# VectorE takes the absolute value in the first step of four batches: an S4D and token-mixing block on one Trainium2 core

## The chip, the cores and the metric

The kernel runs on one core of a Trainium2 chip. The metric is device time in microseconds, the median of several runs. The engines go by the names of the profile: PE is TensorE's matmul and PEld its weight load, DVE is VectorE, ACT is ScalarE, POOL is GpSimd, and SP issues most of the DMAs. Each engine works off its own instructions in program order and waits on semaphores for the others.

## The reference

The block normalizes its input, runs it through a long convolution whose kernel comes from a state-space model (S4D), and then through a token-mixing MLP. Cut to what matters:

```python
def _A_ref(u, log_A_real, A_imag, C_real, C_imag, log_dt, D_skip):   # L = 2048, D = 448, N = 256
    dt = jnp.exp(log_dt)
    A = -jnp.exp(log_A_real) + 1j * A_imag
    C = (C_real + 1j * C_imag) * dt[:, None]
    P = jnp.exp((A * dt[:, None])[:, :, None] * pos[None, None, :])
    K = 2.0 * jnp.einsum("dn,dnl->dl", C, P).real
    Kf = jnp.fft.rfft(K, L2)
    Uf = jnp.fft.rfft(u_t, L2)
    y = jnp.fft.irfft(Uf * Kf[None, :, :], L2)[:, :, :L]
    ...
    return y + u * D_skip[None, None, :]

x = x + ga * _A_ref(layernorm(x) * (1 + ca) + sa, ...)
h = layernorm(x) * (1 + cb) + sb
x = x + gb * mixer(h)        # layernorm, w1 over the tokens, gelu, w2 over the tokens
```

The change lies in the making of K and in the products of the spectra.

## The kernel before

K is made in 56 steps (`NHALF`). A step is one half (128 of the 256 states) of a group of 16 channels. For each step PE makes exponents (`st_exponents`) and later phases, in turns (`st_phase`), each as two PSUM tiles `xe` and `xg` of 128 x 512. ACT takes Exp of the exponents into `mag` (`st_exp`), and sines and cosines of the phases (`st_step`). A cosine is Sin(pi/2 - 2 pi |phase|), so it needs the absolute phase: `ab` from `xe` and one of the three buffers `gs` (`cg_`) from `xg`. Sin of `xe` is written over `xe` itself, after `ab` has been read from it; the cosine of `xe`'s phases goes into `xg`. From these, POOL multiplies the two halves of `G` (L734, L735), and DVE the four quarters of `E`: L736 and L737 with the sine (in the program one half of `E`), L739 and L740 with the cosine (the other half). PE sums `G` times `E` over the states into `kg` (`st_kgen`).

Exp and Sin need different tables on ACT, and a table is loaded by an instruction of its own in front of the first function that needs it. So the steps go in seven batches of 8 (`BATCH`). A batch begins with a window (`window`, from step 40 on `late_window`): eight times Exp, with the next exponents on PE, and other work put in between. Then its eight steps use Sin. The table load for Sin stands in the first step of a batch, behind the two Abs (the first batch loads it at the end of its window). `xe` and `xg` have two buffers each, so the phase of step s + 2 can be made once step s has read its own for the last time (L740).

What else the steps carry:

- `chain(q)` prepares the parameters of 128 channels (the last, q = 3, of 64) as a row of small DVE instructions. `more(n)` issues n of them: in windows by the table `WPACE` (a row for each window, an entry for each of its eight Exp), in steps by `pace`, through `between()`, which stands between the two halves of `E` and first issues what waits in the list `dve`.
- `st_s1` takes finished sums to the first transform on PE (`y1`); its two copies into `yk` go into a list and are issued by `flush`.
- `u_cols` transforms the input's columns for the spectrum (`pu` on PE, `uo` on DVE, then DMAs).
- `piece` works on one piece of the product of spectra: `pc_s2` makes `kx` on PE, `pc_mul` multiplies it on DVE with the input's spectrum `u` into `z` (two instructions, L877), `pc_inv` transforms back on PE (`vv`). In steps 40 and 48, `piece(True)` stands ahead of `st_step` and `piece(False, True)` behind it. `warm` issues ten matmuls on PE whose results nobody reads.

PE, ACT, DVE and POOL run in the order in which the program is written. SP's DMAs are put in order by the tile framework until step 56.

Of the kernel before, what the change touches and what calls it, by code (L numbers as in the profile page):

```python
# [11 lines left out]
F32 = mybir.dt.float32  # L12
F32R = mybir.dt.float32r
BF16 = mybir.dt.bfloat16
AF = mybir.ActivationFunctionType
ALU = mybir.AluOpType
# [6 lines left out]
P = 128  # L23
# [209 lines left out]
def tile_adaln_s4d_mixer(ctx, tc, i, out):  # L233
    nc = tc.nc
    x = i["A_u"][0]
# [17 lines left out]
    with ExitStack() as es:  # L253
        V, S, G, T = nc.vector, nc.scalar, nc.gpsimd, nc.tensor
        tt, ts, stt = V.tensor_tensor, V.tensor_scalar, V.scalar_tensor_tensor
# [126 lines left out]
        def flush(todo):  # L382
            while todo:
                todo.pop(0)()
# [321 lines left out]
        def st_mag2(s):  # L706
            me = v32(mags[s][:, 0])
            w = wp.tile([P, GD], F32, tag="w", name="w")
            G.tensor_tensor(w[:, :, None], me[:, :, 31:32], me[:, :, 1:2], ALU.mult)
            if s in (3, 4, 5):  # L710
                m2 = v32(wm0.rearrange("p k d -> p (k d)")[:, -512 * (s - 2) :][:, 0:512])
            else:
                m2 = m2p[s >= 32 and s % BATCH > 2].tile([P, GD, 32], F32, tag="m2", name="m2")
            G.tensor_tensor(m2, me, w[:, :, None].to_broadcast([P, GD, 32]), ALU.mult)  # L714
            m2s[s] = m2

        def st_step(s, between):
            me, mg_, m2 = v32(mags[s][:, 0]), v32(mags[s][:, 1]), m2s.pop(s)
            E = gp_.tile([P, 2, GD, NJ], F32, tag="E", name="E")
            Gt = gp_.tile([P, 2, GD, NI], F32, tag="G", name="G")  # L720


            xe, xg = phs.pop(s)
            ab, sg, cg_ = (wp.tile([P, 512], F32, tag=nm, name=nm, bufs=b) for nm, b in (("ab", 1), ("gs", 3), ("gs", 3)))

            S.activation(ab, xe, AF.Abs)
            S.activation(cg_, xg, AF.Abs)
            flush(due)
            S.activation(xe, xe, AF.Sin, scale=TWO_PI)
            S.activation(sg, xg, AF.Sin, scale=-TWO_PI)  # L730
            S.activation(cg_, cg_, AF.Sin, scale=-TWO_PI, bias=math.pi / 2)
            S.activation(xg, ab, AF.Sin, scale=-TWO_PI, bias=math.pi / 2)
            se, ce = v32(xe), v32(xg)
            G.tensor_tensor(Gt[:, 1], mg_, v32(sg), ALU.mult)  # L734
            G.tensor_tensor(Gt[:, 0], mg_, v32(cg_), ALU.mult)  # L735
            V.tensor_tensor(E[:, 1, :, 32:64], m2, se, ALU.mult)  # L736
            V.scalar_tensor_tensor(E[:, 1, :, 31::-1], me[:, :, 31::-1], -1.0, se, ALU.mult, ALU.mult)  # L737
            between()
            V.tensor_tensor(E[:, 0, :, 31::-1], me[:, :, 31::-1], ce, ALU.mult)  # L739
            V.tensor_tensor(E[:, 0, :, 32:64], m2, ce, ALU.mult)  # L740
            eg[s] = (E, Gt)
            mags.pop(s)
# [43 lines left out]
        def st_s1(*to):  # L786

            if not ready:
                return False
            p = ready.pop(0)  # L790
            c, gl = divmod(p, NG // 4)
            ks = kss.pop(p)
            y1 = [pms.tile([P, 32, 2, 4, 2], F32, tag="ms", name="y1") for _ in range(2)]
            for o in range(2):
                for m in range(4):
                    for cc in range(2):
                        for q in range(2):
                            r = slice(64 * q, 64 * q + 64)
                            T.matmul(
                                y1[q][64 * cc : 64 * cc + 64, :, o, m], ks[r, o, m], wc[r, cc, r], start=True, stop=True  # L800
                            )

            def out(q, copy):
                o = yks[c][:, :, 2 * gl * GD : 2 * (gl + 1) * GD].rearrange("p k (g q m) -> p k g q m", g=2, q=2)
                copy(o[:, :, :, q], y1[q].rearrange("p k g m b -> p k g (m b)"))

            for q in range(2):
                to[-q].append(partial(out, q, S.copy if to[-q] is act else V.tensor_copy))
            return True
# [259 lines left out]
        def late_window(s):  # L1069

            flush(hold)
            for e in range(BATCH):
                st_exp(s + e)
                if e + 1 < BATCH:
                    st_exponents(s + e + 1)
                else:
                    st_phase(s)
                mellow()
                flush(dve)
                flush(act)  # L1080
                if e == 1:
                    st_kgen(s - 1, dve)
                elif e in (3, 5):
                    piece(False, True)
                st_mag2(s + e)
            st_s1(dve)
            flush(dve)

        def window(s):
            if s:  # L1090
                aside.append(True)
            angle()
            logs(s == 8)
            if s == 8:
                more(10)
                u_scale()
                u_table(0)
                u_table(1)

            if s == 0:  # L1100
                st_exponents(s)
            for e in range(BATCH):
                st_exp(s + e)

                if e + 1 < BATCH:
                    st_exponents(s + e + 1)
                else:
                    st_phase(s)
                mellow()
                flush(dve)  # L1110
                flush(act)
                if s == 8 and e == 0:
                    tt(mod[1], mod[1], mod[2], ALU.mult)
                if s < 32:
                    more(WPACE[s // 8][e])
                if s == 0 and e >= 4:
                    u_stats(e - 4)
                if s == 8 and e in (3, 4):
                    modulation(0, e - 3)
                if s == 8 and e == 5:  # L1120

                    G.tensor_tensor(mod[0], mod[0], mod[2], ALU.mult)
                if s and e < (2 if s <= 32 else 1):
                    st_kgen(s - (2 if s <= 32 else 1) + e)
                elif e == 5 and s < 24:
                    if s == 8:
                        yks[0] = y0.tile([P, 32, DC], F32, tag="yk", name="yk0")
                    st_s1(act)

                for k, e0 in ((4, 1), (5, 3), (3, 6)) if s == 16 else ():  # L1130
                    if e in (e0, e0 + 1):
                        modulation(k, e - e0)

                if s == 8 and e == 0:
                    warm(7)
                if s == 8 and e == 1:
                    u_means()
                if s in (8, 16):
                    some(u_rows, rows, ((0, 2, 2, 2, 2, 0, 2, 2) if s == 8 else (2, 2, 2, 2, 2, 0, 1, 1))[e])
                elif s == 24 and e in (0, 2, 4, 6, 7):  # L1140
                    some(u_cols, cols, 1)

                if s == 0 and e > 1:
                    st_mag2(e - 2)
                elif s and (e < 2 or s >= 32):
                    st_mag2(s + e)
                if s == 0 and e == 3:
                    for r in range(4):
                        dsk_copy(r)
            aside.clear()  # L1150
            if s == 8:
                flush(dve)
            if s >= 24 and st_s1(dve):
                flush(dve)
            if s == 0:

                S.activation(one, one, AF.Sin)

        WPACE = [[0, 2, 2, 1, 1, 1, 1, 1], [2, 2, 2, 2, 1, 3, 3, 1], [4] * 7 + [9], [4] * 8]
        pace = [2] * 5 + [3, 4, 4] + [2] * 24
        for s in range(NHALF):
            if s == 32:
# [32 lines left out]
            if True:  # L1197
                if s < 32 and s % BATCH > 1:
                    st_kgen(s - 2)
                if s % BATCH == 1 or s < 24 and s % BATCH == 0:  # L1200
                    warm(10)
                if (s + 1) % BATCH:
                    st_phase(s + 1)
                elif s + 1 < NHALF:
                    st_exponents(s + 1)
                if s == 7:
                    warm(10)

                due.extend(soon)
                soon.clear()  # L1210
                if s > 32 and s % BATCH:
                    st_kgen(s - 1, soon)
                if s in (40, 48):
                    piece(True)
                    flush(dve)
                st_step(s, between)
                if s in (40, 48):
                    piece(False, True)
# [375 lines left out]
```

## Time and profile before

| | us |
|---|---|
| median of 3 runs | 666.34 |
| lowest, highest | 666.05, 667.45 |
| profiled execution | 666.04 |
| its span | 664.3 |
| last window ends, MLP's first sums begin (about) | 290, 386 |

The profiled execution's span is the time from the first to the last instruction that the profile shows; 1.7 us of its time lie around it. In rows of the order of time, the columns are start, duration, engine, line, operation, tiles, count, and in brackets the idle time of the engine just before and what ended it. A group's row has busy time and mean nanoseconds of one behind the bar, then the idle time ahead of its members.

### The profile page before, as it was taken

Reading aid. Unit: us, or ns where it says so; the run is one execution under the profiler, and the core shown is the slowest. Engines: PE = TensorE matmul, PEld = TensorE weight load, DVE = VectorE, ACT = ScalarE, POOL = GpSimd, SP = SyncE. Lnnn points to the kernel's source line nnn. Section 1 sums busy time; section 2 is a strip of 40 time slices with the busy share of each in tenths; the row PEclk is TensorE's granted clock in tenths of the full one; section 3 lists DMA queues with packets and bytes.
Section 4 is the critical chain, followed back from the end, with each engine's and each line's share of the span. In section 5 each row is a group of like instructions: output and inputs, shape, how many; then the busy total and the mean of one; then the engine's idle time right before and its main releaser. Section 6 shows DMA issues by size and latency. Waiting matters only on the chain.

```text
span 664.3 us, 19155 instructions
## 1 busy us (share of the span) xinstructions
PE 612.2 (92%) x7639; PEld 442.8 (67%) x7639; DVE 444.1 (67%) x852; ACT 440.9 (66%) x828; POOL 269.5 (41%) x350
## 2 busy tenths in 40 slices
PE   1868998999999999999898999999999999999997
PEld 0544455445455555656554667788999999999997
DVE  8999889798893877868665677787522553333331
ACT  6978898999889999999587578886222532222220
POOL 7885597498599788797562000000000000000000
PEclk9999999999999999999999989999999999999999
DMA  6695747598876457676787999946665165555530
GB/s 159 195 222 171 271 136 245 213 269 238 230 263 190 66 160 204 186 210 193 236 279 218 257 241 232 218 117 195 181 179 149 59 197 165 162 160 163 166 113 28
DMA packets 98833, 125.14 MB, mean 188 GB/s; under 512 B 13780, under 2 KB 80120, under 8 KB 98744
## 3 DMA queue, kind: packets, MB, share of 16 engines
q1 hardware_dynamic: 97928, 121.30, 64.6%
q0 software_dynamic: 816, 2.62, 1.6%
q8 instruction: 60, 0.98, 0.7%
q14 instruction: 29, 0.24, 0.1%
HBM read 88.53 MB, written 34.87 MB: 186 GB/s over the span
## 4 chain that ended last, share of the span: by engine, by line
PE 58%; ACT 11%; DMA 10%; DVE 7%; POOL 6%; issue 4%; SPq 2%; DVEq 0%; ACTq 0%; POOLq 0%
PE o L1560 7%; PE o L1562 7%; PE o L1561 7%; PE acc L1397 6%; PE acc L1398 6%; PE acc L1399 6%; PE xe L664 5%; PE kg L761 4%; DMA us_d<-uo 3%; PE xg L664 2%; POOL G L734 2%; DMA w<-in_B_w_dram 2%; POOL G L735 2%; PE vv L892 2%; ACT mag L693 2%
## 5 line engine op out<-in xcount | busy, mean ns | idle before, releaser
L218 ACT CAST whi<-w 128x896 fp32r<-128x896 f32 x64 | 59.7, 939 | 138.6 <-PE o L1561 81.5
L227 DVE TENSOR_TENSOR wlo<-w,whi 128x896 fp32r<-128x896 f32 x64 | 68.1, 1086 | 41.8 <-ACT whi L218 38.7
L734 POOL TENSOR_TENSOR G<-mag,gs 128x512 f32<-128x512 f32 x56 | 71.9, 1284 | 37.4 <-ACT gs L730 37.4
L1397 PE MATMUL acc<-h3h,whi 128*128 128x448 f32 x224 | 83.7, 374 | 3.0 <-ACT h3h L1470 1.4
L1398 PE MATMUL acc<-h3l,whi 128*128 128x448 f32 x224 | 81.9, 365 | 0.4 <-DVE mean L1418 0.2
L1399 PE MATMUL acc<-h3h,wlo 128*128 128x448 f32 x224 | 81.6, 364 | 0.0
L1560 PE MATMUL o<-uh,whi 128*128 128x448 f32 x224 | 81.3, 363 | 0.0
L1562 PE MATMUL o<-uh,wlo 128*128 128x448 f32 x224 | 81.2, 362 | 0.0
L1561 PE MATMUL o<-ul,whi 128*128 128x448 f32 x224 | 80.6, 360 | 0.0
L761 PEld LDWEIGHTS kg<-E,G 128*32 128x32 f32 x3584 | 54.2, 111 | 32.9 <-issue 20.9
L735 POOL TENSOR_TENSOR G<-mag,gs 128x512 f32<-128x512 f32 x56 | 72.0, 1287 | 0.0
L761 PE MATMUL kg<-E,G 128*32 128x64 f32 x3584 | 63.5, 222 | 7.5 <-issue 5.4
L664 PE MATMUL xg<-tab,lph 64*128 64x512 f32 x112 | 62.2, 555 | 7.0 <-DVE E L740 3.0
L1565 DVE TENSOR_TENSOR y<-o,x 128x448 f32<-128x448 f32 x16 | 10.0, 625 | 78.8 <-PE o L1562 78.8
L664 PE MATMUL xe<-tab,lph 64*128 64x512 f32 x112 | 62.2, 555 | 0.4 <-issue 0.4
L714 POOL TENSOR_TENSOR m<-mag,w 128x512 f32<-128x512 f32 x53 | 55.8, 1052 | 4.2
L1397 PEld LDWEIGHTS acc<-h3h,whi 128*128 128x128 f32 x224 | 42.5, 190 | 16.2 <-ACT h L1469 3.5
L1398 PEld LDWEIGHTS acc<-h3l,whi 128*128 128x128 f32 x224 | 42.4, 189 | 3.4 <-DVE h3l L1467 0.5
L1399 PEld LDWEIGHTS acc<-h3h,wlo 128*128 128x128 f32 x224 | 42.4, 189 | 3.3
L1562 PEld LDWEIGHTS o<-uh,wlo 128*128 128x128 f32 x224 | 42.1, 188 | 3.4
L1561 PEld LDWEIGHTS o<-ul,whi 128*128 128x128 f32 x224 | 41.9, 187 | 3.0
L1560 PEld LDWEIGHTS o<-uh,whi 128*128 128x128 f32 x224 | 42.0, 188 | 2.1
(256 smaller groups left out, 1391.5 us busy)
## 6 DMA issues: line engine op xcount, KB each, us to landing
w<-in_B_w_dram SPq DMA_DIRECT2D x64, 224.0 KB
w<-in_B_w_dram SPq DMA_DIRECT2D x32, 448.0 KB
yi<-yu_d SPq DMA_DIRECT2D x32, 224.0 KB
us_d<-uo SPq DMA_DIRECT2D x16, 448.0 KB
u<-us_d SPq DMA_DIRECT2D x64, 112.0 KB
v_d<-vt SPq DMA_DIRECT2D x32, 224.0 KB
vt<-v_d SPq DMA_DIRECT2D x14, 448.0 KB
yu_d<-yt SPq DMA_DIRECT2D x13, 448.0 KB
```

Of the source, the lines that this page charges most:

```text
L218: self.nc.scalar.copy(hi, w)
L227: eng.tensor_tensor(lo, w, hi.bitcast(F32), ALU.subtract)
L664: T.matmul(out[k], lhs[r], rhs[r], start=start, stop=stop)
L734: G.tensor_tensor(Gt[:, 1], mg_, v32(sg), ALU.mult)
L735: G.tensor_tensor(Gt[:, 0], mg_, v32(cg_), ALU.mult)
L761: T.matmul(kg[32 * q : 32 * q + 32, m], Gt[:, c, d], E[:, c, d], start=h == 0 and c == 0 and m == 0, stop=h == 1 and c == 1, skip_group_ch ...
L1397: nc.tensor.matmul(acc[f], hi[:, fs], h3h[:, r], start=r == 0, stop=False)
L1398: nc.tensor.matmul(acc[f], hi[:, fs], h3l[:, r], start=False, stop=False)
L1399: nc.tensor.matmul(acc[f], lo[:, fs], h3h[:, r], start=False, stop=r == 15)
L1560: nc.tensor.matmul(o, hi[:, ks], uh[kh][:, k], start=kh == 0 and k == 0, stop=False)
L1561: nc.tensor.matmul(o, hi[:, ks], ul[kh][:, k], start=False, stop=False)
L1562: nc.tensor.matmul(o, lo[:, ks], uh[kh][:, k], start=False, stop=kh == 1 and k == 6)
```

## The change

In the batches of steps 16, 32, 40 and 48, the absolute phases of the first step are made on DVE, by a bitwise AND of the float's pattern with 0x7FFFFFFF (seen as int32), and no longer by two Abs on ACT. A new function `st_turn` issues the two clears at the end of the window, before the first step. Three things move with it. In the window of step 16 the last entry of `WPACE` goes from 9 to 2, so that five instructions of the chain of the last 64 channels move into the steps. The `flush(dve)` behind `st_s1` at the end of the window of step 32 goes away, and so does the one ahead of `st_step` in steps 40 and 48; what waits in the list there is then issued by `between()`.

```diff
+        turns = {}
+        def turn():
+            return [wp.tile([P, 512], F32, tag=nm, name=nm, bufs=b) for nm, b in (("ab", 1), ("gs", 3), ("gs", 3))]
+        def st_turn(s):
+            turns[s] = turn()
+            for to, x in zip(turns[s][::2], phs[s]):
+                ts(to.bitcast(mybir.dt.int32), x.bitcast(mybir.dt.int32), 0x7FFFFFFF, None, ALU.bitwise_and)
...
             xe, xg = phs.pop(s)
-            ab, sg, cg_ = (wp.tile([P, 512], F32, tag=nm, name=nm, bufs=b) for nm, b in (("ab", 1), ("gs", 3), ("gs", 3)))
-            S.activation(ab, xe, AF.Abs)
-            S.activation(cg_, xg, AF.Abs)
+            if s not in turns:
+                ab, sg, cg_ = turn()
+                S.activation(ab, xe, AF.Abs)
+                S.activation(cg_, xg, AF.Abs)
+            else:
+                ab, sg, cg_ = turns.pop(s)
             flush(due)
             S.activation(xe, xe, AF.Sin, scale=TWO_PI)
...
                 st_mag2(s + e)
+            st_turn(s)
             st_s1(dve)
             flush(dve)
...
             aside.clear()
+            if s in (16, 32):
+                st_turn(s)
             if s == 8:
                 flush(dve)
-            if s >= 24 and st_s1(dve):
+            if s >= 24 and st_s1(dve) and s == 24:
                 flush(dve)
...
-        WPACE = [[0, 2, 2, 1, 1, 1, 1, 1], [2, 2, 2, 2, 1, 3, 3, 1], [4] * 7 + [9], [4] * 8]
+        WPACE = [[0, 2, 2, 1, 1, 1, 1, 1], [2, 2, 2, 2, 1, 3, 3, 1], [4] * 7 + [2], [4] * 8]
...
                 if s in (40, 48):
                     piece(True)
-                    flush(dve)
                 st_step(s, between)
```

The change shifts line numbers: L726 to L740 of before are L737 to L753 in the changed kernel, L805 is L818, L877 is L890, and L726 there is the clear.

On ACT, at the end of the window of step 16, before (with the semaphores for which each waits):

```order
L448 ACTIVATE xa<-A_C_real 128x128 [waits DMAHW1_49,DMAHW2_49,DVE_49,Pool_49]
L448 ACTIVATE ya<-A_C_imag 128x128 [waits DMAHW4_49,DMAHW3_49]
L726 ACTIVATE ab<-xe 128x512 [waits PE_49]
L727 ACTIVATE gs<-xg 128x512 [waits PE_49]
L729 ACT_TABLE_LOAD
L729 ACTIVATE xe<-xe 128x512 [waits Activation_49]
L730 ACTIVATE gs<-xg 128x512
```

and in the changed kernel:

```order
L448 ACTIVATE xa<-A_C_real 128x128 [waits DMAHW1_49,DMAHW2_49,DVE_49,Pool_49]
L448 ACTIVATE ya<-A_C_imag 128x128 [waits DMAHW4_49,DMAHW3_49]
L742 ACT_TABLE_LOAD [waits DVE_49]
L742 ACTIVATE xe<-xe 128x512 [waits Activation_49]
L743 ACTIVATE gs<-xg 128x512 [waits DVE_49]
```

Both Abs are gone, and the wait for DVE's first clear stands ahead of the table load. The other three starts have the same rows.

On DVE, at the same place (the chain's instructions are L454 to L467), before:

```order
L454 TENSOR_TENSOR s<-xa,ya 128x128
L456 TENSOR_TENSOR ya<-ya,xa 128x128
L458 TENSOR_SCALAR s<-s 128x128
L460 RECIPROCAL xa<-s 128x128
L462 TENSOR_TENSOR ya<-ya,xa 128x128
L465 TENSOR_SCALAR t<-s 128x128
L467 SCALAR_TENSOR_TENSOR s<-t,s 128x128
L736 TENSOR_TENSOR E<-m_1968,xe 128x16x32
```

and in the changed kernel:

```order
L454 TENSOR_TENSOR s<-xa,ya 128x128
L456 TENSOR_TENSOR ya<-ya,xa 128x128
L726 TENSOR_SCALAR ab<-xe 128x512
L726 TENSOR_SCALAR gs<-xg 128x512
L749 TENSOR_TENSOR E<-m_1968,xe 128x16x32
L750 SCALAR_TENSOR_TENSOR E<-mag,xe 128x16x32
L458 TENSOR_SCALAR s<-s 128x128
L460 RECIPROCAL xa<-s 128x128
L752 TENSOR_TENSOR E<-mag,xg 128x16x32
```

The clears stand behind two of the chain's instructions; of the other five, two now stand between the halves of `E` in step 16, two in step 17 and one in step 18.

On DVE, at the start of step 40, before:

```order
L805 COPY yk_3662<-y_4644 128x32x2x8
L805 COPY yk_3662<-y_4645 128x32x2x8
L877 TENSOR_TENSOR z_4703<-kx,u 128x448
L877 TENSOR_TENSOR z_4705<-kx,u 128x448
L736 TENSOR_TENSOR E<-m_4497,xe 128x16x32
L737 SCALAR_TENSOR_TENSOR E<-mag,xe 128x16x32
L739 TENSOR_TENSOR E<-mag,xg 128x16x32
L740 TENSOR_TENSOR E<-m_4497,xg 128x16x32
```

and in the changed kernel:

```order
L726 TENSOR_SCALAR ab<-xe 128x512
L726 TENSOR_SCALAR gs<-xg 128x512
L818 COPY yk_3662<-y_4649 128x32x2x8
L818 COPY yk_3662<-y_4650 128x32x2x8
L749 TENSOR_TENSOR E<-m_4497,xe 128x16x32
L750 SCALAR_TENSOR_TENSOR E<-mag,xe 128x16x32
L890 TENSOR_TENSOR z_4718<-kx,u 128x448
L890 TENSOR_TENSOR z_4720<-kx,u 128x448
L752 TENSOR_TENSOR E<-mag,xg 128x16x32
```

The two products `z` go behind the first half of `E`. Step 48 is alike. In step 32 there are no products yet; there the two copies into `yk` stand in the place that `z` has here, between the halves of `E`. PE and POOL keep their order. On SP only loads and stores of this part trade places with their neighbours; the up-row load of `lex` from `pars` is the one that moves furthest.

## The prediction

> **What bounds the kernel now.** I read the page first, then busy time by stretches, then the instructions in order of time around the four batch starts that the change touches, and last the groups by shape, for durations.
>
> ```profile
> span 664.3 us, 19155 instructions
> PE 612.2 (92%) x7639; PEld 442.8 (67%) x7639; DVE 444.1 (67%) x852; ACT 440.9 (66%) x828; POOL 269.5 (41%) x350
> ```
>
> The shares are means over unlike stages. The change lies between 129 and 298 us, so these stretches matter (columns: stretch, length, then busy PE, PEld, DVE, ACT, POOL, clock, DMA share, GB/s):
>
> ```profile
> 133.00:161.00 28.00, 26.06 (x563) 14.37 (x561) 26.45 (x45) 25.93 (x52) 27.47 (x29) 1.00 0.97 264
> 216.50:242.00 25.50, 23.99 (x624) 15.03 (x627) 23.04 (x41) 25.33 (x54) 19.10 (x17) 1.00 0.44 97
> 292.00:318.00 26.00, 24.21 (x652) 15.50 (x652) 23.35 (x42) 25.40 (x54) 19.66 (x17) 1.00 0.67 194
> ```
>
> The batch of step 16 (133 to 161) is bound by POOL: busy 27.47 of 28.00. The batches of steps 32 and 48 (the stretches from 216.5 and 292) are bound by ACT, 25.33 of 25.50 and 25.40 of 26.00, with PE close behind. So microseconds taken from ACT at a batch's start count only if PE and DVE hand over the next phases as much earlier.
>
> **The change, part by part.** Four times, two Abs leave ACT and two clears come to DVE.
>
> ```profile
> L726 ACT ACTIVATE ab<-xe 128x512 f32<-128x512 f32 x56 | 33.8, 604 | 13.9 <-PE xe L664 6.7 <-PE xg L664 6.6
> L805 DVE COPY yk<-y 128x512 f32<-128x512 f32 x19 | 12.3, 684 | 15.3 <-PE y L799 15.2
> L805 ACT COPY yk<-y 128x512 f32<-128x512 f32 x9 | 4.9, 600 | 2.3 <-PE y L799 2.3
> L729 ACT ACT_TABLE_LOAD x6 | 7.7, 1283 | 0.1
> L460 DVE RECIPROCAL xa<-s 128x128 f32<-128x128 f32 x1 | 1.0, 954 | 0.1
> L460 DVE RECIPROCAL xa<-s 128x256 f32<-128x256 f32 x2 | 3.5, 1736 | 0.0
> ```
>
> The trace has no clear of a sign bit. From below it can cost nothing; from above it could run at the rate of the two RECIPROCAL rows, (1736 - 954) / 128 = 6.1 ns an element, so 954 + 384 x 6.1 = 3.3 us. The nearest row is DVE's copy of 128x512 float32 out of PSUM, 684 ns; I take 0.68 us, and 0.60 from start to start as in the pair of copies below.
>
> [...]
>
> What ACT gains is not the 1.1 us of two Abs. Before, the load of the Sin table stood behind both Abs and waited for nothing. Now the program has the wait for the first clear in front of the load, as the rows of the order show, so the load lies behind the clear: clear 0.68, about 0.05 to pass on the semaphore (an estimate from the 0.04 to 0.10 between an end and the next engine's start in the rows below), load 1.28 and 0.02, then Sin. That is 2.03 us from the moment at which DVE can start the clear.
>
> *Step 16.*
>
> ```profile
> 129.27 0.34 ACT L448 ACTIVATE ya<-A_C_imag 128x128 f32<-128x128 f32 x1
> 129.47 0.63 ACT L726 ACTIVATE ab<-xe 128x512 f32<-128x512 f32 x1
> 130.60 1.28 ACT L729 ACT_TABLE_LOAD   x1
> 131.89 0.58 ACT L729 ACTIVATE xe<-xe 128x512 f32<-128x512 f32 x1
> 129.71 0.29 DVE L454 TENSOR_TENSOR s<-xa,ya 128x128 f32<-128x128 f32 x1 [2.06 <-ACT ya L448]
> 130.25 0.22 DVE L458 TENSOR_SCALAR s<-s 128x128 f32<-128x128 f32 x1
> 133.06 1.27 POOL L734 TENSOR_TENSOR G<-mag,gs 128x512 f32<-128x512 f32 x1 [4.13 <-ACT gs L730]
> 163.14 0.29 POOL L401 CAST hl<-A_log_A_real 128x128 fp32r<-128x128 f32 x1 [2.08 <-ACT A_log_A_real L504]
> ```
>
> Two instructions of the chain (L454, L456) stay ahead of the clears on DVE, and L454 waits until ACT's ya is done at 129.61. The first clear therefore takes the place of L458 at 130.25, while ACT could start its Abs at 129.47. Sin: 130.25 + 2.03 = 132.28, against 131.89: **+0.39 us**. POOL's G waits for the Sin behind it (idle 4.13 until 133.06) and then runs without a gap to 161.06 (2.08 before 163.14), so POOL carries the 0.39 to the end of the batch. The five chain instructions that move into steps 16 to 18 (L458 0.22, the reciprocal 0.95, one more immediate operation of 0.22, two tensor operations like L454 of 0.29: 2.0 us) cost nothing beyond that as long as DVE stays behind POOL: DVE is busy 26.45 of 28.00 there, so about 1.5 us is free. That is tight: what sticks out is 0.5 us, and POOL's own shift of 0.39 covers most of it. I count +0.4, with ends 0 and +0.9.
>
> *Step 32.*
>
> ```profile
> 214.13 0.60 ACT L726 ACTIVATE ab<-xe 128x512 f32<-128x512 f32 x1 [0.49 <-PE xe L664]
> 215.23 1.28 ACT L729 ACT_TABLE_LOAD   x1
> 216.53 0.58 ACT L729 ACTIVATE xe<-xe 128x512 f32<-128x512 f32 x1
> 216.42 1.29 DVE L805 COPY yk<-y 128x512 f32<-128x512 f32 x2 [10.16 <-PE y L799]
> 219.41 0.68 DVE L740 TENSOR_TENSOR E<-m,xg 128x512 f32<-128x512 f32 x1
> 220.19 0.46 PE L664 MATMUL xg<-tab,lph 64*128 64x512 f32 x1 [0.73 <-DVE E L740]
> 221.78 0.60 ACT L726 ACTIVATE ab<-xe 128x512 f32<-128x512 f32 x1
> 223.81 0.57 PE L664 MATMUL xe<-tab,lph 64*128 64x512 f32 x1
> 224.91 0.60 ACT L726 ACTIVATE ab<-xe 128x512 f32<-128x512 f32 x1
> ```
>
> The clear can start when the Abs did, 214.13. Sin: 216.16, that is 0.37 earlier. But the two yk copies no longer run while DVE waits for Sin; they stand between E's halves. DVE then has E from 216.80 (Sin ends 216.74), and six operations at 0.60: E, E, yk, yk, E, E. The last starts at 219.80 instead of 219.41 and ends at 220.48. PE's next phase needs exactly that (it idled 0.73 for E L740), so PE starts 0.39 later. It then runs phase, kernel sums, spectrum and the next phase end to end, and the phase of step 35 is ready at 223.81 + 0.57 + 0.39 = 224.77, where ACT would want it at 224.91 - 0.37 = 224.54. With 0.1 to 0.2 until ACT starts, step 35 begins at 224.9, as before. **0 us**, with ends -0.37 and +0.1.
>
> *Steps 40 and 48.*
>
> ```profile
> 250.83 0.57 PE L664 MATMUL xe<-tab,lph 64*128 64x512 f32 x1
> 251.62 0.60 ACT L726 ACTIVATE ab<-xe 128x512 f32<-128x512 f32 x1
> 254.01 0.58 ACT L729 ACTIVATE xe<-xe 128x512 f32<-128x512 f32 x1
> 252.88 1.29 DVE L805 COPY yk<-y 128x512 f32<-128x512 f32 x2 [2.12 <-PE y L799]
> 254.89 1.16 DVE L877 TENSOR_TENSOR z<-kx,u 128x448 f32<-128x448 f32 x2 [0.72 <-PE kx L869]
> 252.76 0.49 PE L664 MATMUL xe<-tab,lph 64*128 64x512 f32 x1
> 253.35 0.58 PE L664 MATMUL xe<-tab,lph 64*128 64x512 f32 x1
> 255.57 1.14 PE L892 MATMUL vv<-z,si 64*64 64x224 f32 x16 [0.72 <-DVE z L877]
> 256.64 1.27 PE L676 MATMUL kg<-ones 128*128 128x256 bf16 x10
> 257.84 0.50 PE L664 MATMUL xe<-tab,lph 64*128 64x512 f32 x1
> 259.56 0.60 ACT L726 ACTIVATE ab<-xe 128x512 f32<-128x512 f32 x1 [0.32 <-PE xe L664]
> 297.51 0.60 ACT L726 ACTIVATE ab<-xe 128x512 f32<-128x512 f32 x1 [0.32 <-PE xe L664]
> ```
>
> The phase is ready at 251.40, so the clear starts at 251.50 and Sin at 253.53, 0.48 earlier. Now E's first half runs before the products z: yk ends its second issue at 254.08, Sin at 254.11, E at 254.15 and 254.75, z at 255.35 instead of 254.89, so 0.46 later. PE has vv behind z (it idled 0.72 for z), the ten warming matmuls behind vv, and the phase of step 42 behind those. All move by 0.46: that phase starts at 258.30 and, now without a wait for E, is ready 0.59 + 0.58 later as at 252.76, at 259.47. ACT, which waited for this phase until 259.56, starts step 42 at about 259.6. **0 us**; what DVE gained waits on PE. Step 48 shows the same wait of 0.32 at 297.51 and is counted alike. Ends for each: -0.48, should PE not hold it, and +0.1.
>
> *SP.* The source moves no load, but one third of a batch's parameter load (lex from pars) changes place three times among SP's other issues. I give it 0: these loads serve exponents of a window some steps later. Ends -0.5 and +1, by one to two of SP's waits.
>
> *Sum* against the profiled execution, 666.04 (span 664.3 and 1.7 around it): +0.4 + 0 + 0 + 0 = 666.4. The median of the three runs lies 0.3 above that execution, so I forecast **666.7 us**.
>
> **The rivals.** *Gains stay.* If PE does not hold steps 32, 40 and 48: +0.39 - 0.37 - 0.48 - 0.48 = -0.9, 665.4. For it speaks ACT's share of 25.33 in 25.50; against it PE's waits of 0.73 and 0.72, which end on the very DVE work that moves.
>
> *The table load does not wait.* If it starts as soon as ACT is free, step 16 has Sin at about 131.0 behind the clear (-0.9), and step 32 has its last E end at 219.28 instead of 220.09, -0.8. Steps 40 and 48 stay where they are, since E sits behind the yk copies. Together -1.7: 664.6. Against it speaks the place of the wait; no load in this trace shows what an open wait in front of it does.
>
> *The clear is slow (slower than before).* An integer view read from PSUM could run below the rate of a copy. Each 0.1 us more than 0.68 delays all four starts alike, since nothing covers them: 0.4 + 4 x (d - 0.68). It is slower by over 0.2% (1.33 us) from d = 0.91 us on, and 677 us at the upper bound of 3.3. For it: two RECIPROCAL rows show that an operation can run at another rate. Against: L458, an immediate operation like this one, takes 0.22 us on 128 columns.
>
> **How the numbers follow.** A measurement of this kernel can tell about 0.2%, 1.33 us, from no change. Forecast (the four starts cancel): 0.55. Gains stay: 0.18, nearly all of it within 0.2%. Load does not wait: 0.12, mostly faster. Slow clear: 0.09. SP's moved issues or a transfer pushed into a busier moment: 0.06, to both sides. Faster takes 0.11 of the third case, 0.01 of the second, 0.03 of the last and 0.03 of the forecast's own ends; slower takes 0.07 of the slow clear, 0.03 of the last and 0.03 of the forecast's ends. So faster 0.18, same 0.69, slower 0.13. The range takes in the first three cases and the bounds of step 16 and of SP, and leaves out most of the slow clear: 664.5 to 668.0.
>
> **What would show it.** In the profile after: at the four starts, ACT idle for about 1.2 us in front of the table load and the load some 0.05 us behind the first clear (if it starts at once, the second rival holds). Clears of 0.68 us. Sin of step 16 at 132.3, of step 32 at 216.5 (0.4 of it from step 16). PE waiting for E L753 at about 220.9 in step 34, and for z in step 40 0.46 us longer. A POOL gap inside the batch of step 16 would show that DVE binds there, and a wait of ACT at step 35 that the gain of step 32 was stopped by PE. I would be wrong if Sin moved forward and the next three batches ended earlier by the same amount.

## The result, and the profile after

| | before | changed |
|---|---|---|
| median of 20 runs, us | 666.41 | 671.28 |
| ratio with its 95% interval | | 1.0057 [1.0033, 1.0080] |
| the same kernel, two later comparisons | | 1.0016 [0.9989, 1.0042], 1.0061 [1.0033, 1.0088] |

The change makes the kernel slower by about 0.5%, some 3 us (the three comparisons give 3.8, 1.1 and 4.1 us; the second can't be told from no change). The forecast was 666.7 us in a range of 664.5 to 668.0; the measured time lies above that range. Three of the changed kernel's 20 executions were slow (749 us, the profiled one, with a mean clock of 0.753, 824 with 0.663 and 1899 with 1.000); here and below such slow executions are left out of the ratios and not of the medians (the other 17 have a median of 670.59), and the profile shown is that of the next comparison (run e1 below). Its page, to be set against the two lines of before:

```profile
span 665.3 us, 19162 instructions
PE 612.1 (92%) x7639; PEld 442.5 (67%) x7639; DVE 450.7 (68%) x860; ACT 435.2 (65%) x820; POOL 269.3 (40%) x350
PEclk9989999989999999999999999999999999999999
```

ACT gave up 5.7 us of work and DVE took 6.6, and this one execution is only 1 us longer than the profiled one of before, at the same mean clock of 0.987. The last line shows a second thing: the granted clock dips in single slices. Each dip read in stretches of 0.1 or 1 us (before, h1 to h4) is 3.41 us at half clock, 0.50, or two of these in a row; here one lies between 137 and 141 us, and the place moves from run to run. So I use a second number of each run, the **clock lost**: (1 - mean granted clock) x span. Over the 316 executions under 690 us whose clock is on record, a fit with one level per kernel and comparison gives 0.72 (+-0.05) us of time for each us of clock lost. That is a mean over all the places at which clock is lost; what it costs at one place has to be read there. Before loses 10 us on average, the changed kernel 12.6.

The clears, the table load and Sin came as forecast. Groups of the changed kernel (busy, mean ns behind the bar):

```profile
L726 DVE TENSOR_SCALAR ab<-xe 128x512 int32<-128x512 int32 x4 | 2.8, 690 | 9.7 <-PE xe L664 9.7
L726 DVE TENSOR_SCALAR gs<-xg 128x512 int32<-128x512 int32 x4 | 2.7, 681 | 0.0
```

Its order of time at step 16 (start, duration, engine, line, and in brackets the idle time just before):

```profile
128.93 0.34 ACT L448 ACTIVATE ya<-A_C_imag 128x128 f32<-128x128 f32 x1
130.67 1.28 ACT L742 ACT_TABLE_LOAD   x1 [1.40 <-DVE ab L726]
160.62 1.28 ACT L498 ACT_TABLE_LOAD   x1
129.91 0.68 DVE L726 TENSOR_SCALAR ab<-xe 128x512 int32<-128x512 int32 x1
133.78 0.70 DVE L458 TENSOR_SCALAR s<-s 128x128 f32<-128x128 f32 x1
134.59 0.95 DVE L460 RECIPROCAL xa<-s 128x128 f32<-128x128 f32 x1
136.00 0.67 DVE L753 TENSOR_TENSOR E<-m,xg 128x512 f32<-128x512 f32 x1
137.79 0.53 DVE L462 TENSOR_TENSOR ya<-ya,xa 128x128 f32<-128x128 f32 x1
138.25 1.29 DVE L465 TENSOR_SCALAR t<-s 128x128 f32<-128x128 f32 x1
136.78 0.46 PE L664 MATMUL xg<-tab,lph 64*128 64x512 f32 x1 [2.34 <-DVE E L753]
137.56 0.98 PE L664 MATMUL xg<-tab,lph 64*128 64x512 f32 x1
```

From ya to the Sin table it is 130.67 - 128.93 = 1.74 us, against 130.60 - 129.27 = 1.33 before: +0.41, where +0.39 was forecast. Then two things are new. L458 and L460 stand between the halves of `E`, so L753 ends 1.3 us later behind the same Sin, and **PE waits 2.34 us for it, where before it waited 1.04**:

```profile
135.41 0.46 PE L664 MATMUL xg<-tab,lph 64*128 64x512 f32 x1 [1.04 <-DVE E L740]
```

And the phase behind that wait takes 0.98 us instead of 0.57: it runs at half clock. Here are the stretches of 4 us at that place, the changed kernel's first, then before's (columns as in the stretches of the prediction; the clock is the third number from the end):

```profile
133.00:137.00 4.00, 1.04 (x7) 0.43 (x5) 3.90 (x7) 4.00 (x10) 3.79 (x5) 1.00 1.08 229
137.00:141.00 4.00, 4.00 (x63) 1.68 (x64) 4.00 (x7) 3.28 (x8) 3.92 (x5) 0.57 1.09 251
141.00:145.00 4.00, 4.00 (x115) 2.42 (x104) 4.00 (x8) 2.69 (x6) 3.79 (x5) 1.00 1.01 255
```

```profile
133.00:137.00 4.00, 2.75 (x20) 1.50 (x20) 3.13 (x6) 4.00 (x9) 3.87 (x5) 1.00 1.06 230
137.00:141.00 4.00, 3.93 (x82) 1.99 (x74) 3.37 (x7) 3.94 (x8) 3.92 (x5) 1.00 1.07 266
141.00:145.00 4.00, 3.92 (x83) 2.02 (x86) 4.00 (x8) 3.70 (x9) 3.92 (x5) 1.00 1.03 264
```

PE is busy 1.04 of 4.00 us, and the next stretch has a clock of 0.57. DVE, which had 0.87 and 0.63 us free at the batch's start, is full from 137 on. The batch ends when ACT loads the next Exp table (L498); before, that row was:

```profile
159.56 1.28 ACT L498 ACT_TABLE_LOAD   x1
```

From the Sin table to that row it is 28.96 us before and 160.62 - 130.67 = 29.95 after: **+0.99 us**, besides the 0.41.

Another engine now holds up the end of the batch. In its last step ACT waited before (first row) for POOL's G, which has to read a buffer `gs` before it is written again, and in the changed kernel it waits for a phase from PE (second row), which PE makes behind a DVE without a gap:

```profile
157.23 0.60 ACT L730 ACTIVATE gs<-xg 128x512 f32<-128x512 f32 x1 [0.60 <-POOL G L734]
156.81 0.60 ACT L737 ACTIVATE ab<-xe 128x512 f32<-128x512 f32 x1 [0.48 <-PE xg L664]
```

POOL's own row of products grew by only 0.35 us: from its first G to the end of its last one it takes 28.35 us (133.13 to 161.48) instead of 28.00.

### The profile page after: what moved, and what is told of

The parts are those of the page before. It is cut to its first block, busy times and chain, and to the rows that moved or that the text cites. A ratio compares the mean times of both kernels' runs of the same rounds, so it can differ in the third digit from the quotient of the medians.

```text
span 746.8 us, 19162 instructions
## 1 busy us (share of the span) xinstructions
PE 709.2 (95%) x7639; PEld 469.0 (63%) x7639; DVE 451.2 (60%) x860; ACT 439.1 (59%) x820; POOL 269.7 (36%) x350
## 4 chain that ended last, share of the span: by engine, by line
PE 82%; DVE 4%; DMA 4%; ACT 4%; POOL 3%; issue 2%; SPq 1%; ACTq 0%; POOLq 0%; DVEq 0%
PE acc L1412 8%; PE xe L664 8%; PE acc L1414 7%; PE kg L774 7%; PE acc L1413 7%; PE o L1577 7%; PE o L1576 7%; PE o L1575 7%; PE vv L905 5%; PE kx L882 4%; PE pu L588 3%; PE y L1449 2%; PE xg L664 2%; PE y L812 1%; POOL G L747 1%
## 5 line engine op out<-in xcount | busy, mean ns | idle before, releaser
L1412 PE MATMUL acc<-h3h,whi 128*128 128x448 f32 x224 | 95.0, 424 | 0.8 <-ACT h3h L1479 0.8
L1414 PE MATMUL acc<-h3h,wlo 128*128 128x448 f32 x224 | 94.2, 421 | 0.0
L1575 PE MATMUL o<-uh,whi 128*128 128x448 f32 x224 | 94.2, 421 | 0.0
L1577 PE MATMUL o<-uh,wlo 128*128 128x448 f32 x224 | 94.2, 420 | 0.0
L1576 PE MATMUL o<-ul,whi 128*128 128x448 f32 x224 | 94.1, 420 | 0.0
L1413 PE MATMUL acc<-h3l,whi 128*128 128x448 f32 x224 | 93.9, 419 | 0.2 <-DVE h3l L1482 0.2
L774 PEld LDWEIGHTS kg<-E,G 128*32 128x32 f32 x3584 | 63.0, 120 | 37.5 <-issue 20.0
L774 PE MATMUL kg<-E,G 128*32 128x64 f32 x3584 | 74.6, 245 | 5.4 <-issue 4.5
L664 PE MATMUL xg<-tab,lph 64*128 64x512 f32 x112 | 70.2, 626 | 6.7 <-ACT gs L743 3.3
L664 PE MATMUL xe<-tab,lph 64*128 64x512 f32 x112 | 69.6, 621 | 0.7 <-DVE t L465 0.7
L1414 PEld LDWEIGHTS acc<-h3h,wlo 128*128 128x128 f32 x224 | 44.2, 197 | 10.5
```

Of the source, the lines that this page charges most:

```text
L664: T.matmul(out[k], lhs[r], rhs[r], start=start, stop=stop)
L774: T.matmul(kg[32 * q : 32 * q + 32, m], Gt[:, c, d], E[:, c, d], start=h == 0 and c == 0 and m == 0, stop=h == 1 and c == 1, skip_group_ch ...
L1412: nc.tensor.matmul(acc[f], hi[:, fs], h3h[:, r], start=r == 0, stop=False)
L1413: nc.tensor.matmul(acc[f], hi[:, fs], h3l[:, r], start=False, stop=False)
L1414: nc.tensor.matmul(acc[f], lo[:, fs], h3h[:, r], start=False, stop=r == 15)
L1575: nc.tensor.matmul(o, hi[:, ks], uh[kh][:, k], start=kh == 0 and k == 0, stop=False)
```

## The experiments

The theories, as the expectations name them. A: the order of work got longer by itself. B: it didn't, and the granted clock is lower. C (after the first four runs): PE's longer wait behind step 16 is what lowers the clock. D (last): the moved chain lengthens the batch of step 16 at any clock, and costs clock besides. Runs of one letter shared a chip and the runs of before. A mean of clock lost is good to 0.4 to 1.1 us.

| run | median us | ratio to before, 95% | clock lost, us |
|---|---|---|---|
| before with e, f, g, h | 667.45, 666.40, 665.95, 666.47 | 1 | 10.0, 9.9, 9.7, 10.6 |
| e1 changed | 668.21 | 1.0016 [0.9989, 1.0042] | 12.6 |
| e2 moves only | 669.60 | 1.0021 [0.9993, 1.0050] | 12.8 |
| e3 clears only | 672.13 | 1.0046 [1.0006, 1.0085] | 14.2 |
| e4 only step 16 | 668.60 | 1.0029 [0.9997, 1.0060] | 12.0 |
| f1 chain paced | 667.36 | 1.0023 [0.9992, 1.0055] | 10.1 |
| f2 clears, paced | 668.01 | 1.0019 [0.9986, 1.0051] | 10.5 |
| f3 chain only | 667.57 | 1.0018 [0.9985, 1.0051] | 12.1 |
| f4 four waits filled | 664.92 | 0.9973 [0.9941, 1.0004] | 7.5 |
| g1 changed | 669.54 | 1.0061 [1.0033, 1.0088] | 13.4 |
| g2 one wait filled | 668.61 | 1.0038 [1.0013, 1.0062] | 10.0 |
| g3 more filled | 668.40 | 1.0037 [1.0010, 1.0063] | 8.7 |
| g4 before, filled | 663.07 | 0.9951 [0.9924, 0.9978] | 7.2 |
| h1 before, one execution | 665.65 | | 10.6 |
| h2 g4 again | 662.96 | 0.9941 [0.9909, 0.9972] | 7.0 |
| h3 g4, late clears | 663.64 | 0.9938 [0.9908, 0.9968] | 5.6 |
| h4 before, early filled | 666.47 | 0.9983 [0.9952, 1.0014] | 9.4 |

**Undoing parts (e).** e1 is the changed kernel. e2 puts the Abs back and leaves the moves: both calls of `st_turn` go. e3 leaves the clears and puts the moves back: `WPACE` and both `flush(dve)` are those of before. e4 is before but for step 16:

```diff
-            if s in (16, 32):
+            if s == 16:
                 st_turn(s)
...
-            st_turn(s)
             st_s1(dve)
             flush(dve)
```

> The changed kernel once more, for a profile at full clock. Theory A (the schedule itself got longer): 668 to 671 us, and the order of time shows a batch that ends 3 to 4 us later with the granted clock at 1.00 in it. Theory B (the order of work costs nothing, the granted clock is lower): the batches last as long as before where the clock is 1.00, and the excess over 666.4 us sits in stretches whose granted clock is below 1; time and mean clock of the runs go together.

> The changed kernel with the absolute phases back on ACT (two Abs in the first step of the four batches, as before), the moved chain instructions, yk copies and products z left where the change puts them. Theory A with the moves at fault: 668 to 671 us as in the changed kernel. Theory A with the clears and the wait in front of the table load at fault: 666 to 667 us. Theory B: whatever the clock of the run gives, 666 us at full clock. By my prediction's steps: steps 40 and 48 lose 0.46 us each for z and win nothing, so 666.4 + 0.9 = 667.3 us.

> The four clears on DVE alone, with the chain's nine instructions in the window of step 16, the yk copies and the products z in their places of before. Theory A with the moves at fault: 665 to 667 us. Theory A with the clears at fault: 668 to 671 us. By the prediction's steps: step 16 has its clear behind all of the chain's seven instructions, 2.0 us later, so about 666.4 + 2.4 = 668.8 us, unless the later batch gives some of it back; steps 40 and 48 then win 0 to 0.48 us each.

> Only the first of the four starts changed: clear and moved chain at step 16, the other three starts as before. By the prediction's steps +0.4 us, 666.8 us. Theory A with step 16 at fault (POOL's batch cut by DVE): 669 to 671 us. Theory A with the late starts at fault: 666 to 667 us. Theory B: 666 to 667 us at the clock of before.

No ratio tells the parts from one another, but the clock does: 12 us or more is lost in all four, and each has something done at step 16. All four profiles show half clock between 136 and 147 us, right behind PE's wait there (2.34, 2.35, 2.60 and 2.34 us). In e3 the clears stand behind all seven chain instructions; its Sin table comes 3.73 us after ya, 2.40 later than before, as the prediction's steps give, and it isn't given back by step 32, whose Exp table comes 78.83 us after ya instead of 74.79.

**Is it PE's idle time (f)?** f1 issues the five chain instructions one a step from step 17, f2 takes the other moves back too, f3 is before with only the chain moved, f4 is the changed kernel with more of the matmuls that nobody reads:

```diff
-        pace = [2] * 5 + [3, 4, 4] + [2] * 24
+        pace = [2] * 5 + [3, 4, 4] + [2] * 8 + [0] + [1] * 5 + [2] * 10
```

```diff
-                    warm(10)
+                    warm({17: 26, 33: 20}.get(s, 10))
...
                 if s in (40, 48):
+                    warm(10)
                     piece(False, True)
```

> The changed kernel, with the five moved chain instructions issued one a step from step 17 to 21, none in step 16. Theory C (what costs is PE's idle time: L458 and L460 between the halves of E in step 16 keep PE waiting 2.34 us instead of 1.04, and the stretch behind such a wait runs at half clock): PE's wait for E in step 17's turn comes back to about 1.1 us, no half clock behind it, the mean clock rises towards that of before (0.985 against 0.981), and the time falls by 1 to 2 us against the changed kernel run again, to 666.5 to 667.5 us. Theory A (DVE in the batch of step 16 is simply too full): the same five instructions cost the same wherever they stand in the batch, 668 us as before them. The late starts keep their longer waits for z.

> The four clears, the chain paced as in f1, and the yk copies and products z in their places of before. Theory C: PE's waits at all four starts are those of before, so clock (0.985) and time (667 +- 1 us beside a before of 667.4) are those of before. If the clears themselves cost clock or time (a lower clock from DVE reading PSUM beside PE, say), it stays at 668 to 670 us.

> The kernel before with one edit: the last entry of the window of step 16 goes from 9 to 2, so the five chain instructions move into steps 16 to 18; no clear. Theory C: PE waits about 2.3 us for E of step 16, the stretch behind it (137 to 141 us) runs at half clock in most runs, 668 to 669 us. Theory A with the clears at fault: 666 to 667 us, as before.

> The changed kernel with more of the matmuls that nobody reads, in PE's idle time at the four starts (26 in place of 10 in step 17, 20 in place of 10 in step 33, 10 more ahead of the transform back in steps 40 and 48). They stand where PE waits for DVE anyway, so at full clock the order of time does not move. Theory C: fewer stretches at half clock, clock up to 0.984 or more, the time 1 to 2 us below the changed kernel run again. Theory A (DVE's order alone): time as the changed kernel, 668 us, or 1 us more where the added matmuls reach past the wait.

For the clock, C holds. With PE's wait back at 1.04 us (f1, f2) the clock lost is 10.1 and 10.5, near that of before; with the chain alone moved (f3) it is 12.1; with the waits filled (f4) 7.5, and f4 comes out at 0.9973. But f1's time didn't fall as C alone wanted. Its order of time:

```profile
131.33 0.34 ACT L448 ACTIVATE ya<-A_C_imag 128x128 f32<-128x128 f32 x1
133.07 1.28 ACT L742 ACT_TABLE_LOAD   x1 [1.40 <-DVE ab L726]
163.42 1.28 ACT L498 ACT_TABLE_LOAD   x1
137.87 0.47 PE L664 MATMUL xg<-tab,lph 64*128 64x512 f32 x1 [1.04 <-DVE E L753]
139.68 0.99 DVE L458 TENSOR_SCALAR s<-s 128x128 f32<-128x128 f32 x1
148.55 1.02 DVE L462 TENSOR_TENSOR ya<-ya,xa 128x128 f32<-128x128 f32 x1
```

The clock is clean here, and the batch lasts 163.42 - 133.07 = 30.35 us, 1.39 more than before: it seems that pacing loses the free time at the batch's start, since none of the five now stands there. So A has a part of its own in batch 16.

**Which wait, and is more to be had (g)?** g1 is the changed kernel; g2 fills only the wait of step 17 (26 matmuls for 10); g3 is f4 with waits of the first batch filled too; g4 is before with such an edit, as many matmuls as its shorter waits hold:

```diff
-                if s % BATCH == 1 or s < 24 and s % BATCH == 0:
-                    warm(10)
+                if s in (3, 4) or s % BATCH == 1 or s < 24 and s % BATCH == 0:
+                    warm({1: 22, 3: 13, 4: 9, 17: 18, 33: 15}.get(s, 10))
...
                 if s in (40, 48):
+                    warm(6)
                     piece(False, True)
```

> The changed kernel a third time, on whatever chip this is, as the base for the three below. Theory C: mean clock about 0.981 and 12 us of clock lost (before: 10), so 1.5 us above before, ratio 1.002. If the change costs something else besides (the first comparison had 1.0057), the ratio comes out above 1.004 at that same clock.

> The changed kernel with 26 in place of 10 of the unread matmuls in step 17 alone, in PE's wait behind the first step of batch 16. Theory C with step 16 as the place: no half clock at 137 to 141 us, 1.5 to 2 us less clock lost than the changed kernel, time as before or up to 1 us below. If the later starts (waits of 1.3 to 1.5 us at steps 32, 40, 48) carry the loss, the clock stays at 0.981.

> The changed kernel with the added matmuls of f4 and, besides, 22 in place of 10 in step 1, 13 in step 3 and 9 in step 4, where PE waits 1.2 to 1.7 us for ACT and DVE. Theory C: fewer half-clock stretches near 32, 38 and 48 us, so 5 to 7 us of clock lost and 664 to 665 us, the fastest so far. If a half clock near 48 comes from the 3.6 us at 44.8 to 48.4 us, in which PE waits for nothing that the profile shows, that one stays.

> The kernel before with added matmuls in the same places, as many as its shorter waits hold (22, 13 and 9 in steps 1, 3 and 4, 18 in step 17, 15 in step 33, 6 more in steps 40 and 48). Theory C: its clock rises as well, and it comes out equal to g3 within 1 us, since at equal clock the change is worth nothing. If the clears on DVE are worth something once the clock is even, g3 is faster than this by more than 1 us.

g2 gives back the clock of before by 16 matmuls in one place (13.4 to 10.0 us lost), but not the time that was expected with it: its ratio is 1.0038 [1.0013, 1.0062]. Taken together, the kernels with the long wait at step 16 (the changed kernel, e2, e3, e4, f3) lose 12.6 (+-0.3) us of clock, f1, f2 and g2 10.2 (+-0.4), before 10.0 (+-0.2). g2's stretches, to be set against those of the changed kernel above:

```profile
133.00:137.00 4.00, 2.73 (x24) 1.90 (x21) 3.90 (x7) 4.00 (x9) 3.92 (x5) 1.00 1.07 233
137.00:141.00 4.00, 3.39 (x82) 1.82 (x80) 4.00 (x7) 3.19 (x7) 3.92 (x5) 1.00 1.08 264
```

and from its order of time:

```profile
136.38 0.47 PE L664 MATMUL xg<-tab,lph 64*128 64x512 f32 x1 [1.27 <-ACT gs L743]
130.27 1.28 ACT L742 ACT_TABLE_LOAD   x1 [1.40 <-DVE ab L726]
160.24 1.28 ACT L498 ACT_TABLE_LOAD   x1
```

The clock stays at 1.00, yet the batch lasts 160.24 - 130.27 = 29.97 us, as in e1: the 1 us there is DVE's. And the half-clock stretch of e1 is not paid in this batch. Step 19 starts later for it (first row e1, second g2):

```profile
142.62 0.60 ACT L737 ACTIVATE ab<-xe 128x512 f32<-128x512 f32 x1 [1.31 <-PE xg L664]
141.53 0.60 ACT L737 ACTIVATE ab<-xe 128x512 f32<-128x512 f32 x1 [1.03 <-PE xe L664]
```

Counted from the Sin table, that is 11.95 us against 11.26; step 20 starts after 15.21 against 15.26, so nothing of it is left. f1 and f2 say the same: the batch lasts 30.35 us at full clock (f1) and 30.34 with a half-clock stretch in it (f2). Two stretches in a row may cost something there: f3 has two and lasts 30.91 us, e2, with the same work in this batch and one stretch, 29.98. So C explains where clock is lost and not why the batch got longer. g3 missed: it loses less clock than g2 and isn't faster. g4 was expected equal to g3 and is 0.9% below it; what held g3 back wasn't found (beside f4 it has only the matmuls of steps 1, 3 and 4, which do g4 no harm).

**What was left open, and the faster version (h).** h1 is before for a second profile, h2 is g4 again, h3 is g4 with the clears of steps 32, 40 and 48 (the rest in before's order), h4 is before with the matmuls of steps 1, 3 and 4 alone.

> The kernel before, for a second profile of it. Theory D (the five chain instructions lengthen batch 16 whatever the clock, and the longer wait of PE in it costs clock besides): from ACT's ya of step 16 to the Exp table of the next window 30.29 us as in the first profile and in g4, with no half clock between 137 and 141 us. If that time or that half clock comes and goes with the run, it shows 31.5 us or a half clock there as well.

> g4 again. If its 0.9951 is the added matmuls' doing: again 0.993 to 0.998 of before, clock 0.987 or more. If it was a lucky chip or hour: 0.999 to 1.002.

> g4 with the clears of steps 32, 40 and 48 on DVE, yk copies and z in their places of before, and step 16 left alone. By the prediction's steps for these starts (what ACT gains waits on PE and DVE): equal to h2 within 1 us. If the clears at the late starts are worth something when batch 16 is not lengthened: 1 us or more below h2.

> The kernel before with the added matmuls of steps 1, 3 and 4 alone. If the gain of g4 comes from the early half-clock stretches (near 32 and 38 us): as h2, 0.995 to 0.997. If from those at the four batch starts: 0.998 to 1.001.

ACT's order of time in h1:

```profile
130.94 0.34 ACT L448 ACTIVATE ya<-A_C_imag 128x128 f32<-128x128 f32 x1
132.28 1.28 ACT L729 ACT_TABLE_LOAD   x1
161.25 1.28 ACT L498 ACT_TABLE_LOAD   x1
```

h1's batch lasts 28.97 us, so before's length is no accident of one run. Over all profiles: 28.96 or 28.97 in four of the six with the chain in its old place and in the window's order (29.67 and 29.78 in h4 and h2, where PE stands still for 1.54 and 1.01 us within a row of matmuls and waits for nothing that the profile shows), 29.94 to 30.91 in the ten with the chain moved. h3 equals h2 within 0.7 us: the late clears bring and cost nothing that these runs can tell. h2 and h3 are the **fastest versions**, 0.6% below before; h4 shows that the early matmuls alone give little of it (0.9983, in an interval that reaches past 1). The page of h3:

```profile
span 661.6 us, 19275 instructions
PEclk9999899999999999999999999999999999999999
```

## Why the prediction failed

*The clears, the wait in front of the load, Sin of step 16*: right. 0.68 us was 0.69 and 0.68; +0.39 was +0.41; the rivals of the slow clear and of the load that doesn't wait fell.

*Steps 32, 40 and 48*: right in the main, gain and loss both, as the changed kernel's order of time shows:

```profile
216.92 0.69 DVE L726 TENSOR_SCALAR ab<-xe 128x512 int32<-128x512 int32 x1 [7.99 <-PE xe L664]
218.99 0.58 ACT L742 ACTIVATE xe<-xe 128x512 f32<-128x512 f32 x1
222.66 0.68 DVE L753 TENSOR_TENSOR E<-m,xg 128x512 f32<-128x512 f32 x1
227.73 0.60 ACT L737 ACTIVATE ab<-xe 128x512 f32<-128x512 f32 x1 [0.17 <-PE xg L664]
254.49 0.69 DVE L726 TENSOR_SCALAR ab<-xe 128x512 int32<-128x512 int32 x1 [0.88 <-PE xe L664]
256.55 0.58 ACT L742 ACTIVATE xe<-xe 128x512 f32<-128x512 f32 x1
258.44 1.15 DVE L890 TENSOR_TENSOR z<-kx,u 128x448 f32<-128x448 f32 x2
259.11 1.14 PE L905 MATMUL vv<-z,si 64*64 64x224 f32 x16 [1.33 <-DVE z L890]
262.66 0.60 ACT L737 ACTIVATE ab<-xe 128x512 f32<-128x512 f32 x1 [0.89 <-PE xg L664]
```

Both profiles have a half-clock stretch near step 32 (at 0.50 from 213.2 to 216.6 us before, between 215 and 220 after), and the phase of step 32 is taken up 10.07 and 10.19 us after the start of the Exp table's load, against 9.70 in h2, whose stretch begins only at 220.6 us. Counted from the clear's start (before: the first Abs at 214.13), Sin of step 32 comes after 2.07 us instead of 2.40, L753 after 5.74 instead of 5.28, and step 35 after 10.81 instead of 10.78: gain 0.33, loss 0.46, nothing left. From the phase of step 40 (ready 0.14 us ahead of the clear, at 254.35; before at 251.40), Sin comes after 2.20 instead of 2.61, z after 4.09 instead of 3.49, and step 42 after 8.31 instead of 8.16: z is 0.60 later where 0.46 was forecast, and 0.15 is lost where 0 was. Step 48 is alike (its step 50 comes after 8.32 instead of 8.16). The rival that the gains stay fell, and h3 beside h2 says the same in time.

*The step that failed* is the sentence that the five chain instructions "cost nothing beyond that as long as DVE stays behind POOL: DVE is busy 26.45 of 28.00 there, so about 1.5 us is free". It was wrong in its sizes and in its condition, and beside it stand two terms that the sum had at nothing.
1. The 2.0 us of durations came from rows in a window in which POOL was idle. Beside POOL's products, L458 took 0.70 us for 0.22, L462 0.53 for 0.29, L465 1.29 for 0.22 and L467 0.39 for 0.29; L460 stayed at 0.95. Together 3.86 us for 1.97. That POOL's products are the cause is my reading of these rows; no run took POOL's work away, so it is not shown.
2. The free 1.5 us was a mean over a stretch. It lay in the first 8 us, in waits for Sin, and behind 141 us DVE was full even before. The batch became 0.99 us longer, beyond the 0.41; where the forecast had +0.9 as upper end for step 16, 1.4 came. The condition failed with it: DVE did not stay behind POOL. POOL's row grew by 0.35 us only, and what ends the batch now is ACT, which waits for PE's phases behind DVE.
3. PE's wait was priced only by what stands behind it; the sum had no term for the clock. A wait of 2.34 to 2.60 us at this place has half clock behind it in six of six profiles, one of at most 1.27 us in two of eleven. So the changed kernel loses 12.6 us of clock (mean of 11.7, 12.6 and 13.4) instead of 10. At the fit's mean price that would be about 2.5 x 0.72 = 1.8 us of time. But 1.7 us of the clock lost is the stretch behind step 16 itself, and g2 beside e1 shows that this one isn't paid in its batch. What is left, 0.8 us of clock, is 0.6 us by the fit.
4. The batch of step 24 has no term in the sum. From its Sin table to the Exp table of step 32 it takes 206.73 - 174.53 = 32.20 us in e1 and 30.82 in g1, against 204.06 - 174.98 = 29.08 and 30.21 in the two profiles of before. ACT waits there for POOL's G, 2.43 us in e1 and 1.01 in g1, against none and 0.40; POOL in turn waits for a store of the chain's rows into `pars` to land (4.38 and 2.88 us, against 2.16 and 1.72). The rows of ACT, two of e1 and then one of before:

```profile
181.98 0.60 ACT L743 ACTIVATE gs<-xg 128x512 f32<-128x512 f32 x1 [2.43 <-POOL G L747]
206.73 1.28 ACT L693 ACT_TABLE_LOAD   x1
204.06 1.28 ACT L693 ACT_TABLE_LOAD   x1
```

The item *SP* of the prediction is not settled by this. In the changed kernel SP issues a load of `lex` from `pars` about 7 us ahead of that store (at 167.7 and 174.6 us in e1), which it doesn't there in before; the prediction gave 0 to such moved loads. But h3, without that load there, has the wait too (2.73 us on ACT), and e4, with it, hardly (0.25), and no run moves the load alone. What makes the store late stays open.

As far as the traces show, the loss lies between steps 16 and 32. From ya of step 16 to the Exp table of step 32 it is 77.80 us in e1 and 76.47 in g1, against 74.79 and 74.57 in before: 1.7 to 3.2 us more, 1.4 of it in the batch of step 16. From there to the table that ACT loads ahead of the MLP's sums it is 158.76 and 159.05, against 159.53 and 159.12: nothing more. The three ratios average 1.0045, 3.0 us. How these 3 us split beyond the 1.4 is not shown: at equal clock, by the fit, the ten kernels with the chain moved stand -0.4 to +3.7 us (g3) from the before of their call, 0.9 on average. And the 0.2% that the prediction took as what a comparison can tell was too small: the same two kernels came out at 1.0016 and at 1.0061.

## What to carry to other kernels

Here a wait of PE of 2.34 us or more at step 16 had a stretch at half clock behind it in six of six profiles: look at the granted clock behind such a wait. Whether that costs time is read from who waits for that stretch: here one stretch held up step 19 by 0.7 us and was made good by step 20. Filling such waits with matmuls that nobody reads can be worth more than the reordering of work around them (0.6% in h2 and h3, for lines that compute nothing; in g3 it gave no time). Take an instruction's duration from a place with the same neighbours (L458 took 0.22 us with POOL idle and 0.70 beside POOL's products), and an engine's free time from the stretch in which the work would land, not from a mean over a batch. And ask which engine will hold up the end of a batch after the change, not which one does before it.

## What the runs showed of the hardware

Half clock, 0.50 in the profile, comes in stretches of 3.41 us (213.16 to 216.58 in before) or two of them in a row (6.83 us from 212.5 in h1), and where they begin shifts from run to run: at 32.3, 49.3, 213.2, 363.4 and 387.2 us in before, at 48.6, 69.1, 212.5 and 366.0 in h1, the same kernel. Behind PE's wait at step 16 there was one each time that the wait took 2.34 us or more (six of six profiles), and in two of eleven where it took at most 1.27. PE's busy share doesn't tell it by itself: in before, PE is shown busy for 3.40 of 3.40 us from 209.8 to 213.2, with 11 matmuls one after another, and the next 4 us have a clock of 0.58. What sets the clock beyond that, no run shows.
